# Row tile 2 of a transformer block: x loaded earlier and transposed by DMA, row tile 3 through ScalarE's queue, first Q weights behind two transposes, two transpose banks as accumulators

## The chip, the cores and the metric

The kernel runs on one core of a Trainium2 chip. The time is the device time of one execution in microseconds (us); executions of one kernel in one batch can differ by up to 2 us (the kernel before, batch 2: 690.77 to 692.77), and the 95% intervals below reach about 0.8 us to either side, so with five rounds a difference of about 1 us in 691 can just be told from none. For every run I also look at the mean clock that was granted to TensorE (1.0 is full speed).

## The reference, cut to what matters

```python
def _layernorm(x, axis=-1, eps=1e-5): ...
x = A_x                                              # 2048 x 1024, bf16
h = x + attention(_layernorm(x) @ wqkv) @ wo         # 32 heads, causal, window of 256
h2 = h + silu(_layernorm(h) @ w1) @ w2               # hidden size 3584
```

The change touches only the beginning: the normalization of the first 512 rows ("block 0", four row tiles of 128) and their projection to V, before their projection to Q and K.

## The kernel before: the parts that matter

The matmuls of this kernel read the normalized rows in transposed form (`lhsT=lnT_b[0]...`), so the rows have to be transposed first. A V group is eight matmuls of 512 columns, one for each K tile (128 of the 1024 columns of x), that add up in one accumulator bank; the root of a tile is the square root in its normalization, on ScalarE. For block 0 the kernel transposes row tiles 0, 1 and 2 on TensorE (`turn_first`) so as to start early, and tile 3 by a DMA transpose (`ln_transpose`). Tiles 0 and 1 are multiplied before they are normalized in full and scaled afterwards; their normalized form, which Q and K need, is transposed a second time, by DMA.

```python
def ln_transpose(xt, dst, j):                       # DMA transpose, issued by SyncE
    nc.sync.dma_start_transpose(out=dst[:, :, j * P:(j + 1) * P], in_=xt)

# loads, in the order in which they are issued
load_x(0, 0)
load_x(0, 1, nc.scalar)
load_wqkv(2 * D, 4, (nc.sync, nc.scalar))            # first V weights, four quarters
load_x(0, 2)
load_wqkv(2 * D + 512, 2)                            # second V weights, two halves
load_x(0, 3)
load_wqkv(0)                                         # first Q weights, 1 MB
...
v_group(0, 0, 0, hold, place({...}))                 # V, tile 0, transposes of 0 and 1 in between
turn_first(1, 3, x_mid[1], dve)
...
v_group(0, 1, 0, hold)                               # V, tile 1
pair = [next_acc() for _ in range(2)]                # V, second half of tiles 0 and 1
for k in range(0, KT, 4):
    for j in range(2):
        for kt in range(k, k + 4):
            if k and j:
                turn_first(2, kt - k, x_ring[2], act)    # tile 2 transposed on TensorE
                ...
            nc.tensor.matmul(pair[j], ...)
...
for j in (3, 0, 1):
    ln_transpose(x_ring[j], lnT_b[0], j)
for c0 in (D, 512, D + 512):
    load_wqkv(c0)                                    # the other Q and K weights
v_group(0, 2, 0, act); v_group(0, 2, 1, act)         # V, tile 2
v_group(0, 3, 0, act); v_group(0, 3, 1, act)         # V, tile 3
# then qk_group(0, ...): Q and K of block 0, which read all four tiles
```

Two terms recur below. An issue is the time in which an engine's sequencer hands a transfer to a queue; a landing is the time at which the transfer's semaphore is complete. SyncE's queue takes both the loads and the DMA transposes, in the order of the code.

The softmax here doesn't subtract the row's maximum and nothing guards it: scores larger than these inputs give would overflow.

## Time and profile before

| what | value |
|---|---|
| time, median of 3 runs | 691.15 us (691.08 to 691.35) |
| span of the profiled execution | 688.9 us, granted clock 1.000 (device time 690.64, a fast one) |
| Q/K projections of block 0 start | 21.09 us |
| first Q weights: issued, landed | 6.95, 13.80 us |
| DMA transpose of tile 3: issued, landed | 14.65, 17.50 us |
| of tile 0 | 16.11, 18.83 us |
| of tile 1 | 17.43, 20.20 us |
| next 1 MB of weights: issued, landed | 18.75, 24.21 us |

How to read it: TensorE is busy from one end to the other, so the question for any change here is when the Q/K projections can start; from there on nothing is different. The last thing that they need is the transpose of tile 1, and it lands 0.9 us before they begin. The lines themselves stand in the prediction. One line that I looked up there but did not use as I should have is shown here; it is the view of transfers in a short stretch, with the operation, KB and the median time from issue to landing:

```profile
r_w<-in_A_wqkv_dram SPq DMA_DIRECT2D x1, 1024.0 KB, 5.5
```

A megabyte of weights with no other load in front of it, issued at 18.75 behind tile 1's transpose (landed at 20.20), took 5.5 us to land.

### The profile page before, as it was taken

To read this page: it belongs to the slowest core of one execution; us is meant where nothing else is said; L and a number is where in the kernel's file an instruction comes from. 1 tells how busy PE (TensorE), PEld (TensorE's weight loads), DVE (VectorE), ACT (ScalarE), POOL (GpSimd) and SP (SyncE) were. 2 spreads that over 40 slices of the span, in tenths; PEclk is the share of its full clock that TensorE was granted. 3 is DMA by queue.
4 is the path that set the end of the run, shared out by engine and by line. 5 is a ranking of instruction groups with operands and counts; after the bars stand their busy time and mean duration, and the time that the engine had idled before them with its cause. 6 is when DMAs were issued, how large, how long until landed. Compare 5 with 4: busy or idle time off the path is not lost.

```text
span 688.9 us, 14243 instructions
## 1 busy us (share of the span) xinstructions
PE 685.2 (99%) x6011; PEld 342.3 (50%) x6011; DVE 291.2 (42%) x613; ACT 244.2 (35%) x464; POOL 160.8 (23%) x295
## 2 busy tenths in 40 slices
PE   9999999999999999999999999999999999999998
PEld 4445555555555555544444444444444444444445
DVE  5267647744444449444316133342233251333111
ACT  7326666666667666421300033300133100233000
POOL 1006666566666656400000000000000000000000
PEclk9999999999999999999999999999999999999999
DMA  7832231126241889871023310022300123100110
GB/s 259 275 64 69 40 85 57 25 63 186 71 131 21 257 252 272 199 267 40 23 88 112 84 39 0 1 91 70 85 0 1 21 96 90 39 1 1 30 39 24
DMA packets 78641, 61.48 MB, mean 89 GB/s; under 512 B 52465, under 2 KB 62705, under 8 KB 78577
## 3 DMA queue, kind: packets, MB, share of 16 engines
q1 hardware_dynamic: 77888, 59.78, 30.2%
q8 instruction: 47, 0.77, 0.4%
q10 hardware_dynamic: 688, 0.79, 0.3%
q14 instruction: 18, 0.14, 0.1%
HBM read 39.85 MB, written 8.39 MB: 70 GB/s over the span
## 4 chain that ended last, share of the span: by engine, by line
PE 99%; DVE 0%; issue 0%
PE hacc L669 19%; PE hacc L706 18%; PE acc L250 17%; PE acc L706 11%; PE acc L669 9%; PE acc L240 7%; PE acc L271 7%; PE o_ps L383 5%; PE sc L303 3%; PE hacc L271 2%; PE sc L355 1%; PE o_ps L240 1%; PE o_ps L167 1%; PE sc L329 1%; PE acc L525 0%; PE o_ps L525 0%
## 5 line engine op out<-in xcount | busy, mean ns | idle before, releaser
L373 POOL TENSOR_SCALAR_AFFINE_SELECT r_e<-r_e 128x512 bf16<-128x512 bf16 (+1 forms) x288 | 157.8, 563 | 123.9 <-ACT r_e L363 60.8
L706 PEld LDWEIGHTS <-r_a 128*128 128x128 bf16 x952 | 90.9, 98 | 103.0
L669 PEld LDWEIGHTS <-r_w 128*128 128x128 bf16 x896 | 87.3, 98 | 104.8
L706 PE MATMUL hacc<-r_a 128*128 128x512 bf16 (+2 forms) x616 | 122.5, 360 | 0.0
L669 PE MATMUL hacc<-r_e,r_w 128*128 128x512 bf16 x456 | 100.9, 379 | 0.0
L315 ACT ACTIVATE r_e<-sc 128x768 bf16<-128x768 f32 x96 | 78.2, 814 | 47.9 <-PE sc L303 47.9
L678 ACT ACTIVATE r_n<-hacc 128x512 f32<-128x512 f32 x30 | 17.9, 597 | 178.9 <-PE hacc L669 178.9
L250 PEld LDWEIGHTS <-r_w 128*128 128x128 bf16 x512 | 47.1, 98 | 55.0 <-issue 1.0
L706 PE MATMUL acc<-r_a 128*128 128x512 bf16 x336 | 74.0, 379 | 0.0
L252 DVE CAST r_a<-acc 128x512 bf16<-128x512 f32 x56 | 38.7, 692 | 57.7 <-PE acc L250 57.4
L250 PE MATMUL acc<-r_t,r_w 128*128 128x512 bf16 x256 | 59.6, 380 | 0.0
L250 PE MATMUL acc<-r_w 128*128 128x512 bf16 x256 | 57.8, 380 | 0.0
L383 PEld LDWEIGHTS <-r_e 128*128 128x128 bf16 x1440 | 47.4, 96 | 17.9
L669 PE MATMUL acc<-r_e,r_w 128*128 128x512 bf16 x216 | 49.1, 379 | 0.0
L271 PE MATMUL acc<-r_o,r_a 128*128 128x512 bf16 x208 | 48.7, 380 | 0.0
L383 PE MATMUL o_ps<-r_a,r_e 128*128 128x33 bf16 x1440 | 48.1, 178 | 0.0
L721 DVE SCALAR_TENSOR_TENSOR r_t<-hacc,r_t 128x512 bf16<-128x512 f32 (+2 forms) x22 | 14.0, 635 | 56.7 <-PE hacc L706 56.7
L316 ACT ACTIVATE r_e<-sc 128x256 bf16<-128x256 f32 x96 | 37.6, 392 | 0.0
L271 PEld LDWEIGHTS <-r_a 128*128 128x128 bf16 x256 | 23.4, 98 | 26.9
L721 DVE SCALAR_TENSOR_TENSOR r_t<-acc,r_t 128x512 bf16<-128x512 f32 x12 | 8.3, 692 | 64.2 <-PE acc L706 64.2
L679 DVE SCALAR_TENSOR_TENSOR r_a<-r_n,hacc 128x512 bf16<-128x512 f32 x30 | 20.6, 687 | 33.0 <-ACT r_n L678 33.0
L669 PE MATMUL hacc<-r_a,r_w 128*128 128x512 bf16 x144 | 33.0, 379 | 0.0
(100 smaller groups left out, 539.6 us busy)
## 6 DMA issues: line engine op xcount, KB each, us to landing
r_w<-in_B_w_dram SPq DMA_DIRECT2D x8, 896.0 KB, 5.2
r_a<-in_B_w_dram SPq DMA_DIRECT2D x7, 1024.0 KB, 7.5
r_w<-in_A_wqkv_dram SPq DMA_DIRECT2D x4, 1024.0 KB, 7.8
h_dram<-r_t SPq DMA_DIRECT2D x16, 256.0 KB, 3.1
r_t<-h_dram SPq DMA_DIRECT2D x16, 256.0 KB, 2.8
out_dram<-r_t SPq DMA_DIRECT2D x31, 128.0 KB, 1.7
r_o<-in_A_x_dram SPq DMA_DIRECT2D x15, 256.0 KB, 4.6
r_e<-h_dram SPq DMA_DIRECT2D x3, 1024.0 KB, 5.7
```

The lines of the kernel that those rows point to most:

```text
L240: nc.tensor.matmul(acc, lhsT=lnT_b[b % 2][:, kt, j * P:(j + 1) * P], rhs=wv[:, kt, c * 512:(c + 1) * 512], start=(kt == 0), stop=(kt == KT ...
L250: nc.tensor.matmul(acc, lhsT=wqk[:, kt, col0:col0 + P], rhs=lnT_b[b % 2][:, kt, :], start=(kt == 0), stop=(kt == KT - 1))
L252: copy(out=(qT, kT)[which][b][:, g, :], in_=acc)
L271: nc.tensor.matmul(acc, lhsT=qT[b][:, g, j * P:(j + 1) * P], rhs=wo[:, g, c * 512:(c + 1) * 512], start=(g == 0), stop=(g == G - 1))
L303: nc.tensor.matmul(sc[hh // 2][half * 64:half * 64 + 64, hh % 2, col:col + qb - qa], lhsT=kT[t // 4][r0:r0 + DH, g, k0:k0 + 64], rhs=qT[b] ...
L315: nc.scalar.activation(out=tri[:, :, :, 64:256], in_=both, func=ACT.Exp, scale=scale)
L316: nc.scalar.activation(out=e[:, 1024:1280].rearrange("p (h q) -> p h q", q=P), in_=bank[:, :, 192:320], func=ACT.Exp, scale=scale)
L373: nc.gpsimd.affine_select(out=dst, in_=src, pattern=[[0, n] for n in dst.shape[1:-1]] + [[sgn, P]], compare_op=ALU.is_ge if upper else ALU ...
L383: nc.tensor.matmul(o_ps[pair][:, qt * 2 + hh, 0:VW], lhsT=chunk_of(i, bank, piece, pair, hh), rhs=v[:, b * 4 + kt, g * 4 + pair * 2 + hh, ...
L669: nc.tensor.matmul(acc, lhsT=w1[:, kt, ft * P:(ft + 1) * P], rhs=ln2T[b][:, kt, :], start=(kt == 0), stop=(kt == KT - 1))
L706: nc.tensor.matmul(acc[:, 0:c1 - c0], lhsT=gT[:, ft, j * P:(j + 1) * P], rhs=w2[ft // 4][:, ft % 4, c0:c1], start=(ft == 0), stop=(ft == F ...
L721: nc.vector.scalar_tensor_tensor(out=t_out[j % 2][:, c0:c1], in0=acc[:, 0:c1 - c0], scalar=0.5, in1=t_in[j % 2][:, c0:c1], op0=ALU.mult, o ...
```

## The change

The intent is to take the eight transposes of tile 2 off TensorE, to have tile 2 and tile 3 ready sooner, and to spread the accumulators of the V groups over more banks. For this, x of tile 2 goes ahead of the third quarter of the first V weights on SyncE's queue (the second and fourth go through ScalarE's); tile 3's x is loaded through ScalarE's queue, after tile 2's root; the first Q weights move behind the transposes of tiles 2 and 3 on SyncE's queue. The copies of tile 1's transposes go from VectorE to ScalarE.

```diff
-    load_wqkv(2 * D, 4, (nc.sync, nc.scalar))
-    load_x(0, 2)
+    load_wqkv(2 * D, 4, (nc.sync, nc.scalar), load_x)    # x of tile 2 after the second quarter
     load_wqkv(2 * D + 512, 2)
-    load_x(0, 3)
-    load_wqkv(0)
 ...                                                      (helper changes cut)
+    def turn_root():
+        turn(1, 1)
+        ln_root(st, rs, 2)
+        load_x(0, 3, nc.scalar)
 ...
-    turn_first(1, 3, x_mid[1], dve)
+    turn(1, 3)
+    ln_recip(rs, 2)
+    ln_norm(x_ring[2], st, rs, 2)
+    ln_transpose(x_ring[2], lnT_b[0], 2)
 ...                                                      (statistics of tile 3 moved up, cut)
+    ln_norm(x_ring[3], st, rs, 3)
+    ln_transpose(x_ring[3], lnT_b[0], 3)
+    load_wqkv(0)
     v_group(0, 1, 0, hold)
     scaled(0)
     scaled(1)
+    acc_banks += [t[:].bitcast(F32) for t in tp_ps[2:]]
+    acc_n[0] = 2
     pair = [next_acc() for _ in range(2)]
 ...
-                if k and j:
-                    turn_first(2, kt - k, x_ring[2], act)
 ...
-    for j in (3, 0, 1):
         ln_transpose(x_ring[j], lnT_b[0], j)              # now in the loop over tiles 0 and 1
```

More of the change, by code (lines that the diff above doesn't have):

```diff
@@ L135, in load_x, with load_wqkv @@
         queue.dma_start(out=x_ring[(b % 2) * 4 + j], in_=x2d[(b * 4 + j) * P:(b * 4 + j + 1) * P, :])
-    def load_wqkv(c0, parts=1, queues=(nc.sync,)):
+    def load_wqkv(c0, parts=1, queues=(nc.sync,), second=None):
         dst = wqk[:, :, c0:c0 + 512] if c0 < 2 * D else wv[:, :, c0 - 2 * D:c0 - 2 * D + 512]
@@ L141, in load_wqkv @@
             queues[k // n % len(queues)].dma_start(out=dst[:, k:k + n, :], in_=wqkv_v[:, k:k + n, c0:c0 + 512])
+            if second and k == n:
+                second(0, 2)
     warm = view(r_e, 0, P)
@@ L479, in place @@
     def place(at):
-        return lambda kt: turn_first(*at[kt], x_mid[at[kt][0]], (act, dve)[at[kt][0]]) if kt in at else None
+        return lambda kt: at[kt]() if kt in at else None
     acc_banks += [o[:].rearrange("p a b -> p (a b)") for o in o_ps]
@@ L496 @@
     nc.vector.tensor_tensor(out=mean[:, 2:3], in0=mean[:, 0:1], in1=mean[:, 1:2], op=ALU.add)
-    turn_first(0, 0, x_mid[0], act)
-    turn_first(0, 1, x_mid[0], act)
+    ln_stats(x_ring[2], st, 2)
+    turn = lambda j, h: turn_first(j, h, x_mid[j], act)
+    turn(0, 0)
+    turn(0, 1)
     for i in range(2):
         busy(2)
-    v_group(0, 0, 0, hold, place({1: (0, 2), 3: (0, 3), 5: (1, 0), 6: (1, 1), 7: (1, 2)}))
-    turn_first(1, 3, x_mid[1], dve)
+    def turn_root():
+        turn(1, 1)
+        ln_root(st, rs, 2)
+        load_x(0, 3, nc.scalar)
+    v_group(0, 0, 0, hold, place({1: lambda: turn(0, 2), 3: lambda: turn(0, 3), 5: lambda: turn(1, 0), 6: turn_root, 7: lambda: turn(1, 2)}))
+    turn(1, 3)
+    ln_recip(rs, 2)
+    ln_norm(x_ring[2], st, rs, 2)
+    ln_transpose(x_ring[2], lnT_b[0], 2)
     for j in range(2):
@@ L506 @@
         root_first(j)
-    ln_stats(x_ring[2], st, 2)
-    ln_root(st, rs, 2)
+    ln_stats(x_ring[3], st, 3)
+    ln_root(st, rs, 3)
     ln_recip(rs, 0)
     ln_recip(rs, 1)
-    ln_recip(rs, 2)
-    ln_norm(x_ring[2], st, rs, 2)
+    ln_recip(rs, 3)
+    ln_norm(x_ring[3], st, rs, 3)
+    ln_transpose(x_ring[3], lnT_b[0], 3)
+    load_wqkv(0)
     v_group(0, 1, 0, hold)
@@ L519 @@
             for kt in range(k, k + 4):
-                if k and j:
-                    turn_first(2, kt - k, x_ring[2], act)
-                    if kt == k:
-                        ln_stats(x_ring[3], st, 3)
-                        ln_root(st, rs, 3)
                 nc.tensor.matmul(pair[j], lhsT=lnT_b[0][:, kt, j * P:(j + 1) * P], rhs=wv[:, kt, 512:1024], start=(kt == 0), stop=(kt == KT - 1))
-    norm_first(0)
-    norm_first(1)
-    ln_recip(rs, 3)
-    ln_norm(x_ring[3], st, rs, 3)
     for j in range(2):
+        norm_first(j)
         nc.scalar.activation(out=v[:, j, 16:32, 0:DH], in_=pair[j].rearrange("p (h d) -> p h d", d=DH), func=ACT.Identity, scale=rs[:, j:j + 1])
-    for j in (3, 0, 1):
         ln_transpose(x_ring[j], lnT_b[0], j)
```

## The prediction

> **What bounds the kernel now.** I read the page first: busy time by engine and the chain that ended last.
>
> ```profile
> PE 685.2 (99%) x6011; PEld 342.3 (50%) x6011; DVE 291.2 (42%) x613; ACT 244.2 (35%) x464; POOL 160.8 (23%) x295
> ...
> PE 99%; DVE 0%; issue 0%
> ```
>
> TensorE is busy in 685.2 of 688.9 us and the chain is TensorE from end to end, at a granted clock of 1.000. So any time that the change saves or adds on TensorE's stream passes to the end one for one, and nothing on another engine counts unless TensorE waits for it. The diff only touches the first 21 us (row block 0: V projection and its transposes), about 3% of the time. I therefore went on to TensorE's timeline there (start, duration, both in us; matmuls overlap, so I use starts and not durations).
>
> ```profile
> 6.92 0.59 PE L240 MATMUL acc<-r_w 128*128 128x512 bf16 x2
> 7.35 0.28 PE L218 MATMUL tp<-ident,r_e 128*128 128x128 bf16 x2
> 7.46 0.38 PE L240 MATMUL acc<-r_w 128*128 128x512 bf16 x1
> 7.68 0.28 PE L218 MATMUL tp<-ident,r_e 128*128 128x128 bf16 x2
> 7.91 0.38 PE L240 MATMUL acc<-r_w 128*128 128x512 bf16 x1
> ...
> 8.56 1.89 PE L240 MATMUL o_ps<-r_w 128*128 128x512 bf16 x8
> 10.29 1.03 PE L525 MATMUL o_ps<-r_w 128*128 128x512 bf16 x4
> ...
> 12.88 0.28 PE L218 MATMUL tp<-ident,r_o 128*128 128x128 bf16 x2
> 12.99 0.38 PE L525 MATMUL acc<-r_w 128*128 128x512 bf16 x1
> ...
> 14.19 1.89 PE L240 MATMUL acc<-r_w 128*128 128x512 bf16 x8
> ...
> 21.09 27.79 PE L250 MATMUL acc<-r_w 128*128 128x512 bf16 x128
> ```
>
> What to see: eight 512-wide matmuls take 10.29 - 8.56 = 1.73 us, 0.216 each. The eight transposes of row tile 2 (the r_o ones) lie between the last four matmuls before 14.19. The Q/K projections begin at 21.09, and they need all four row tiles transposed.
>
> Then SyncE's queue, because it orders the loads and the DMA transposes.
>
> ```profile
> 1.26 0.93 SPq L141 DMA_DIRECT2D r_w<-in_A_wqkv_dram  x2
> 2.23 0.47 SPq L135 DMA_DIRECT2D r_o<-in_A_x_dram  x1
> 2.74 1.37 SPq L141 DMA_DIRECT2D r_w<-in_A_wqkv_dram  x2
> 4.97 0.34 SPq L135 DMA_DIRECT2D r_o<-in_A_x_dram  x1
> 6.95 0.37 SPq L141 DMA_DIRECT2D r_w<-in_A_wqkv_dram  x1
> 14.65 4.04 SPq L206 DMA_TRANSPOSE r_w<-r_o  x3
> 18.75 1.87 SPq L141 DMA_DIRECT2D r_w<-in_A_wqkv_dram  x3
> ```
>
> The three transposes cost the queue 1.35 us each; the view of landings gives 2.9, 2.8 and 2.7 us from issue to landing, so the last lands at about 17.4 + 2.7 = 20.1, before 21.09. In between, the DMA engines' share in 40 slices of 14.5 to 21.0 us shows the data of each as a burst of six slices of 0.16 us, about 0.95 us, starting 1.3 us after its issue:
>
> ```profile
> DMA  0000000008999990049999940299999600962935
> ```
>
> **What the Trainium skill says.** "DMA: Bandwidth & Descriptors", section "Queues, rings and completion order": on one DMA engine the descriptors of one queue are taken in ring order. The trace agrees as far as landings go: pieces of SyncE's queue issued at 1.75, 2.23 and 2.74 land at 7.0, 7.8 and 9.15. The same page, "Issuing engines are not separate DMA queues": issuing from ScalarE saves only the sequencer's time, the data share the same 16 engines; here the engines move some 385 GB/s without a gap from 2.5 to 13.3 us whichever queue issues, so a load only comes earlier by pushing another later. "VectorE: DVE Perf Modes", "The three transpose paths", gives 390 ns for a 128x128 transpose on TensorE and 1309 ns by DMA. This trace has a far smaller TensorE figure in the stream (below), and that one decides. "TensorE: Matmul & The Clock Gate", "Wait — 56ns, not 53.3ns?", gives 55.6 and 215.7 ns from start to start for 128 and 512 columns on a warm array; the trace agrees (12.88 to 12.99 for two transposes, 0.216 for a matmul).
>
> **The change part by part.**
>
> 1. Transposes of tile 2 leave TensorE. From 12.88 to 14.19 are 1.31 us; four matmuls alone are 4 x 0.216 = 0.86. Saved: 0.45 us, on the path. This is all that can be gained in steady flow.
>
> 2. x tile 2 goes ahead of the third quarter of the first V weights (K tiles 4 and 5) in SyncE's queue. Both are 256 KB. Before, that quarter is issued at about 1.75 and lands 5.2 later, at 7.0; x tile 2 at 2.23 and 5.6 later, 7.8. Swapped, the quarter lands at 7.8. TensorE reaches K tile 4 at 7.13 (the second of the pair at 6.92), so it now waits until about 7.83: +0.70. Before, it lost 0.12 later, at 7.91, waiting for the last quarter (the two transposes from 7.68 are over at 7.79; that quarter lands at 1.99 + 5.9 = 7.9), and this wait is swallowed. Net +0.58: the second V group starts at 9.14 instead of 8.56.
>
> 3. The eight copies of transposed tiles 0 and 1 are all on ScalarE (0.37 us each, 0.30 to 0.33 back to back). The last four, with the root of tile 2 (0.29), run from about 8.37 to 10.0. The second V group reads the third copy at its K tile 4 (9.14 + 0.86 = 10.0; copy done 9.67) and the fourth at 10.44 (done 10.0). No wait, margin about 0.3.
>
> 4. Row tile 2: x lands at 7.0, statistics 1.5 us on VectorE, root, reciprocal, normalization (0.55) until about 10.0; the DMA transpose then lands at about 12.9. Its group starts at 9.14 + 8 x 0.216 + 16 x 0.216 = 14.33 (before 14.19). No wait. The extra accumulators keep that group from waiting for an eviction, which before was no wait either.
>
> 5. Row tile 3: the new order on ScalarE puts its root after the two squares (1.28 each) and roots, at about 13.0; normalized by 13.9, so its transpose is issued at 13.95 rather than 14.65 and lands at 16.85. Needed at 14.33 + 3.46 = 17.79. No wait.
>
> 6. The first Q weights, 1 MB, are issued at 6.95 before, and now only after tile 3's transpose, at 13.95 + 1.26 = 15.2, ahead of the transposes of tiles 0 and 1. At 385 GB/s they occupy the engines for 2.7 us, from about 16.55 (1.35 after issue, as the load at 18.75 had it) to 19.3. The two transposes behind them in ring order take 0.95 each: 21.15, and landing another 0.4: about 21.55. TensorE, without a wait, would want the Q/K projections at 14.33 + 32 x 0.216 = 21.24. So it waits some 0.3, and with a little for the semaphore starts at about 21.65 to 21.7.
>
> Sum: 21.7 - 21.09 = +0.6 us; put by parts, -0.45 + 0.58 + 0.45. After that TensorE runs as before: the next weights (issued around 18.4) are wanted 6.9 us later and land by 25, and x of block 1 comes near 32 us, where VectorE has over 2 us of slack. 691.15 + 0.6 = 691.75.
>
> **Rivals.** (a) Only the quarter's wait exists: the transposes mix with the Q weights or the transfer is quicker than I think, and tile 1 lands in time: -0.45 + 0.58, 691.3. For it: the margin in step 6 is 0.3 us, less than the error of my start times. Against it: the total data ahead of the last transpose is fixed by ring order. (b) Only the late Q weights matter: if TensorE didn't wait at K tile 4, everything up to the transposes moves 0.58 forward and about 0.4 of wait remains at the Q/K start: 691.1. Against it: the first V group was already following the landings to within 0.2 us. (c) Neither wait: 690.7, the intent of the change. (d) Transposes and copies disturb one another more than by bytes, or tile 3 comes late for its group: another 0.5 to 1 us, 692.3 to 692.8.
>
> **Range and chances.** Most weight lies on my sum and (a); the range 690.7 to 692.6 covers (a) to the mild form of (d). 2% would be 13.8 us. All that the change can move is the first 21 us, and the waits named are below 1 us each, so within 2% has 0.98.
>
> **What would show it.** In the changed profile: no transposes of r_o on TensorE; a gap of 0.6 to 0.7 us before the fifth matmul of the first V group, released by the weights' DMA; second V group at 9.1; tile 2's group at 14.3 with no DMA wait; the Q/K start at 21.6 to 21.7 with a wait released by a DMA transpose; from there the same distance to the end. It is wrong if the quarter lands before 7.2, if the Q/K start is at 21.0 or sooner, or if the time between Q/K start and the end changes by more than 0.3 us.

## The result, and the profile after

| | before | after |
|---|---|---|
| time, median, same rounds | 691.19 us (690.87 to 691.47, 6 runs) | 693.49 us (692.91 to 695.53, 6 runs) |
| ratio | | 1.0037, 95% interval 1.0024 to 1.005 |

A ratio is the mean time of one kernel's fast runs over that of the other's in the same rounds, so it is not quite the ratio of the medians quoted. The interval lies clear of 1: the change costs 2.3 us, and 693.49 lies outside the predicted range of 690.7 to 692.6. So the size was wrong: 0.6 us expected, 2.3 measured.

The page of the changed kernel, busy time and chain:

```profile
PE 686.1 (99%) x6003; PEld 342.0 (49%) x6003; DVE 290.0 (42%) x609; ACT 244.1 (35%) x464; POOL 160.8 (23%) x295
...
PE 98%; DMA 2%; SPq 0%; ACT 0%; issue 0%; DVE 0%
```

TensorE runs eight instructions fewer (the transposes are gone), and yet DMA now stands in the chain with 2%. That is where to look. TensorE's timeline in the first part (start, duration in us, what it is, and in brackets the idle time before it with what ended it):

```profile
7.17 0.38 PE L239 MATMUL acc<-r_w 128*128 128x512 bf16 x1
8.55 0.38 PE L239 MATMUL acc<-r_w 128*128 128x512 bf16 x1 [1.00 <-DMA r_w<-in_A_wqkv_dram]
...
9.86 1.89 PE L239 MATMUL o_ps<-r_w 128*128 128x512 bf16 x8
...
15.04 1.89 PE L239 MATMUL tp<-r_w 128*128 128x512 bf16 x8
...
20.22 1.89 PE L239 MATMUL o_ps<-r_w 128*128 128x512 bf16 x8
24.10 29.47 PE L249 MATMUL acc<-r_w 128*128 128x512 bf16 x128 [1.99 <-DMA r_w<-r_o]
```

There are two waits. The first (1.00) is for the quarter of V weights that x of tile 2 overtook. The second (1.99) stands in front of the Q/K projections and is released by a DMA transpose. And there is a third thing that the prediction had not thought of: the 128 matmuls of that first Q/K stretch last 29.47 us, against 27.79 before. The view of windows says why (columns: stretch, its length, busy time of the five engines with their instructions, granted TensorE clock, DMA share, GB/s):

```profile
24.10:26.00 1.90, 1.90 (x6) 0.76 (x7) 0.00 (x0) 0.00 (x0) 0.00 (x0) 0.62 1.05 369
26.00:28.00 2.00, 2.00 (x6) 0.70 (x5) 0.00 (x0) 0.58 (x1) 0.00 (x0) 0.51 1.09 385
28.00:30.00 2.00, 2.00 (x11) 0.93 (x10) 0.49 (x1) 0.00 (x0) 0.00 (x0) 1.00 1.09 377
```

After the wait the granted clock falls to one half for about 3.4 us and then returns. That costs 29.47 - 27.79 = 1.7 us in this execution, which was the slowest of the six (695.53); the other five show a clock of 1.0 and lie between 692.91 and 693.61. So the drop does not make the median. The transfers do. SyncE's queue (start and duration of the issues):

```profile
10.78 5.20 SPq L205 DMA_TRANSPOSE r_w<-r_o  x2
16.03 0.57 SPq L141 DMA_DIRECT2D r_w<-in_A_wqkv_dram  x1
16.79 5.09 SPq L205 DMA_TRANSPOSE r_w<-r_o  x2
21.93 2.85 SPq L141 DMA_DIRECT2D r_w<-in_A_wqkv_dram  x3
```

The order is that of the code: tiles 2 and 3, Q weights, tiles 0 and 1. The transfers that begin between 16.0 and 16.9 take, from issue to landing (last number of each line):

```profile
r_w<-in_A_wqkv_dram SPq DMA_DIRECT2D x1, 1024.0 KB, 6.0
r_w<-r_o SPq DMA_TRANSPOSE x1, 6.3
```

The Q weights take 6.0 us where I had put 4.5, and the transpose of tile 0 behind them 6.3 where a free one takes 2.7 to 2.9. The profiled execution had a late start besides (its first x tile landed at 4.06, not 3.52). I therefore ran the changed kernel again.

### The profile page after: what moved, and what is told of

It is laid out like the page before. It is cut to its first block, busy times and chain, and to the rows that moved or that the text cites.

```text
span 693.8 us, 14223 instructions
## 1 busy us (share of the span) xinstructions
PE 686.1 (99%) x6003; PEld 342.0 (49%) x6003; DVE 290.0 (42%) x609; ACT 244.1 (35%) x464; POOL 160.8 (23%) x295
## 3 DMA queue, kind: packets, MB, share of 16 engines
q10 hardware_dynamic: 832, 1.05, 0.4%
## 4 chain that ended last, share of the span: by engine, by line
PE 98%; DMA 2%; SPq 0%; ACT 0%; issue 0%; DVE 0%
PE hacc L674 19%; PE hacc L711 17%; PE acc L249 17%; PE acc L711 10%; PE acc L674 9%; PE acc L270 7%; PE acc L239 7%; PE o_ps L382 5%; PE sc L302 3%; PE hacc L270 1%; DMA r_w<-in_A_wqkv_dram 1%; PE sc L354 1%; DMA r_w<-r_o 1%; PE sc L328 1%; PE tp L534 0%; PE tp L239 0%
## 5 line engine op out<-in xcount | busy, mean ns | idle before, releaser
L249 PE MATMUL acc<-r_w 128*128 128x512 bf16 x256 | 59.5, 388 | 2.0 <-DMA r_w<-r_o 2.0
```

What stands on the lines that cost most here:

```text
L249: nc.tensor.matmul(acc, lhsT=wqk[:, kt, col0:col0 + P], rhs=lnT_b[b % 2][:, kt, :], start=(kt == 0), stop=(kt == KT - 1))
```

## The experiments

All outputs are right. Four batches ran; the kernel before had medians of 691.01, 691.25, 690.97 and 691.48 us in them, and every ratio is to the runs of before of the same batch.

### e0: the changed kernel again (batch 2)

No edit.

> The changed kernel once more, on the same chip as the three below: about 693.4 at a clock of 1.000. If the wait of 2 us at the Q/K start makes the clock drop in a share of the executions, some show 0.997 and 695 to 695.5; if the drop of the first profile was chance, none do.

Measured: 693.83 us (693.46 to 694.24, 5 runs), ratio 1.0033 (1.002 to 1.0046), clock 1.0 in every run. The Q/K line of its timeline:

```profile
23.91 27.79 PE L249 MATMUL acc<-r_w 128*128 128x512 bf16 x125 [2.11 <-DMA r_w<-r_o]
```

At full clock (27.79, as before) the wait is still there: the loss of 2.3 to 2.6 us comes without any drop of the clock. This clean execution gives the balance. The second V group starts at 9.55 (before 8.56): +0.99, of which 0.23 is there before the overtaken quarter plays a part (the first V matmul at 6.11, before 5.88). From there to tile 2's group at 14.73 are 5.18 us, before 5.63: -0.45. From there to the Q/K start are 9.18 us; the four groups need 6.91 of them (8 x 4 x 0.216), which was all they took before: +2.27. Together +2.81, and the Q/K start moved by 23.91 - 21.09 = 2.82.

### e7: only the place of the Q weights (batch 2)

```diff
     ln_transpose(x_ring[2], lnT_b[0], 2)
+    load_wqkv(0)
 ...
     ln_transpose(x_ring[3], lnT_b[0], 3)
-    load_wqkv(0)
```

> The changed kernel with only the first Q weights moved, to between the transposes of tiles 2 and 3; x tile 2 stays ahead of the weights' quarter. Theory L: the wait at the Q/K start (2.0 us in the profile) goes; a wait of some 0.5 us for tile 3's transpose, which now stands behind the 1 MB, comes; the quarter's wait of 1.0 stays: 691.9 to 692.4. Were the Q weights harmless there, 693.4 would stay.

Measured: 691.84 us (691.34 to 692.45, 5 runs), ratio 1.0006 (0.9994 to 1.0017). Its timeline around the Q/K start:

```profile
18.65 1.90 PE L239 MATMUL acc<-r_w 128*128 128x512 bf16 x8 [0.41 <-DMA r_w<-r_o]
20.39 1.89 PE L239 MATMUL o_ps<-r_w 128*128 128x512 bf16 x8
22.12 8.15 PE L249 MATMUL acc<-r_w 128*128 128x512 bf16 x36
```

No wait is left in front of the Q/K projections; a smaller one, 0.41 us, appears before tile 3's group, whose transpose now goes behind the load. One line moved, and 693.83 - 691.84 = 2.0 us of the loss are gone. All other parts of the change, gains and losses together, come to the 0.6 us that are left (691.84 - 691.25; the interval includes none), about what I had predicted for the whole.

### e2: the kernel before, with only the Q weights late (batch 1)

```diff
     load_x(0, 3)
-    load_wqkv(0)
 ...
     for j in (3, 0, 1):
         ln_transpose(x_ring[j], lnT_b[0], j)
+        if j == 3:
+            load_wqkv(0)
```

> The kernel before with only the first Q weights moved to between tile 3's transpose and those of tiles 0 and 1. Theory L: the whole loss and more appears, since tile 3's transpose is issued at 14.65 as in the changed kernel's profile (14.75): last transpose lands near 24, the Q/K start moves from 21.1 to about 23.5 to 24, 693.6 to 694.1 us. Rival S: 691.2 to 691.8, no more than my predicted byte count (2.7 us on the wire plus two transposes) gives.

Measured: 695.94 us (694.73 to 697.83, 6 runs), ratio 1.0069 (1.0056 to 1.0083); five of the six runs show a clock of 0.995 to 0.998, and the one at 1.0 is the fastest, 694.73.

```profile
24.83 5.40 PE L249 MATMUL acc<-r_w 128*128 128x512 bf16 x17 [3.21 <-DMA r_w<-r_o]
```

The late load alone makes the kernel before slower by 3.7 us at full clock (694.73 - 691.01, a single execution against a median), more than I had expected. The wait was 3.21 us; the load took 6.43 us and the transpose of tile 1 landed at 24.70. So the move makes a loss without the rest of the change, as e7 shows that the rest makes hardly any without the move.

### e10: the kernel before, with only x of tile 2 ahead (batch 2)

```diff
-    load_wqkv(2 * D, 4, (nc.sync, nc.scalar))
-    load_x(0, 2)
+    load_wqkv(2 * D, 4, (nc.sync, nc.scalar), load_x)
```

> The kernel before with only x tile 2 moved ahead of the third quarter of the first V weights. My step 2 (the two pieces of 256 KB swap places, +0.58 us): 691.6 to 691.8. If the quarter is delayed by more than its bytes, as the gap of 1.0 to 1.5 us in the changed kernel's and the first run's profile suggests: 692.0 to 692.4. If the swap costs nothing: 691.1.

Measured: 691.79 us (691.36 to 692.22, 5 runs), ratio 1.0005 (0.9993 to 1.0017). The difference of medians is 0.54, the predicted one was 0.58. The interval includes zero, so the size is consistent with step 2 rather than proved by the times. In the trace, the wait for the overtaken quarter is 0.64 us, but another of 0.48 us, for the quarter before it, comes first, and the second V group starts at 9.61, 1.05 us later than in the profile of before. That is more than the medians show: single executions differ here by as much as the effect.

### e5: the Q weights behind all four transposes (batch 2)

```diff
     ln_transpose(x_ring[3], lnT_b[0], 3)
-    load_wqkv(0)
 ...
-    for c0 in (D, 512, D + 512):
+    for c0 in (0, D, 512, D + 512):
```

> The changed kernel with the first Q weights issued after all four transposes. The transposes then land by about 20 us and the Q/K start waits for the weights alone. Theory ramp (loads from HBM run slowly for their first 1.5 us or so when none ran before, whatever stands behind them): 1 MB issued near 18.6 lands near 24.3, as late as now, 693.2 to 693.8. Theory mix (the load was slow because transposes were being issued and queued behind it): 2.7 us on the wire, lands near 23.1, 692.2 to 692.6.

Measured: 695.25 us (693.78 to 696.22, 6 runs), ratio 1.005 (1.0037 to 1.0064). Two runs have a clock of 1.0 (693.78 and 693.86), four 0.997 or 0.998.

```profile
24.29 3.47 PE L249 MATMUL acc<-r_w 128*128 128x512 bf16 x8 [2.39 <-DMA r_w<-in_A_wqkv_dram]
```

The executions at full clock and the landing fit the theory of the ramp. Now the releaser is the load itself: issued at 18.74, landed at 24.24, 5.50 us, as the load of 18.75 in the kernel before. All four transposes have landed long before (tile 1's at 20.18, 1.4 us after the load's issue). So the load is slow even with no transpose behind it, and with transposes behind it 0.6 us slower still (6.14 in e0).

### e13: no pause in the loads before it (batch 3)

A theory for the slow load: no load had been running for a while, so it starts cold. Here two x tiles of block 1 are loaded just ahead of it, through ScalarE's queue.

```diff
     ln_root(st, rs, 3)
+    load_x(1, 0, nc.scalar)
+    load_x(1, 1, nc.scalar)
 ...
-    for j in range(4):
+    for j in range(2, 4):
         load_x(1, j)
```

> The changed kernel with two of the four x loads of block 1 (512 KB) moved from after the weights to ScalarE's queue right after the root of tile 3, so that loads from HBM are flowing when the first Q weights start. If the slow start is due to the pause in loads before it, those weights land in about 4.5 us from issue instead of 6.1, and the Q/K start moves about 1.3 us forward: 692.2 to 692.7. If it is due to something else (the weights' own addresses, the transposes before), landing stays near 6 us and the time at 693.5 or above.

Measured: 694.32 us (692.99 to 696.17, 4 runs, two of them at a clock of 0.998 or less), ratio 1.0046 (1.0027 to 1.0065). The Q weights took 6.10 us, and the Q/K start is where it was:

```profile
23.87 6.42 PE L249 MATMUL acc<-r_w 128*128 128x512 bf16 x29 [1.93 <-DMA r_w<-r_o]
```

Of the four executions the two at full clock took 692.99 and 693.52. The two x loads landed at 16.10 and 16.93, so loads were flowing when the weights were issued at 15.74, and the landing came no sooner for it. The start did change: from 17.5 to 19.0 us the engines moved 210 to 283 GB/s (61 to 231 in e0), and a later dip took the gain away. The pause is not what makes the landing late; whether it has a part in the slow start stays open.

### e15: another megabyte in the same place (batch 4)

As e7, with the four x loads of block 1 (1 MB in all) where the Q weights had been.

```diff
     ln_transpose(x_ring[2], lnT_b[0], 2)
+    load_wqkv(0)
 ...
     ln_transpose(x_ring[3], lnT_b[0], 3)
-    load_wqkv(0)
+    for j in range(4):
+        load_x(1, j)
```

> The changed kernel with the first Q weights between the transposes of tiles 2 and 3 (as in e7, 691.8), and the four x loads of block 1 (also 1 MB, in rows of 2 KB) put where the late Q weights were, ahead of the transposes of tiles 0 and 1. Theory A: any 1 MB load issued there takes 6 us and holds the transposes behind it up: the transpose of tile 1 lands at 23.5 to 24, Q/K projections start at 23.6 to 24 after a wait of 1.5 to 2 us, about 693.6. Rival B: only the 1 KB pieces of the weights, or one large load, start slowly: the loads land about 4.5 us after issue, the transpose of tile 1 by 22, Q/K start at about 22.2, 691.8.

Measured: 693.49 us (693.33 to 694.13, 5 runs), ratio 1.003 (1.0018 to 1.0043), clock 1.0 throughout.

```profile
23.63 27.79 PE L249 MATMUL acc<-r_w 128*128 128x512 bf16 x125 [1.49 <-DMA r_w<-r_o]
```

The time and the wait are those of theory A. The x loads, issued from 15.52 to 17.09, land at 19.08, 19.96, 20.56 and 21.50, and the transpose of tile 1 at 23.49. What costs is a megabyte in that place, not these weights. But the x loads are late for another reason than the Q weights were. They stood behind the Q weights (landed at 17.45) and tile 3's transpose (18.46), and once these were through they moved at full rate within about a microsecond (last column GB/s):

```profile
18.00:18.50 0.50, 0.15 (x1) 0.00 (x0) 0.00 (x0) 0.31 (x1) 0.00 (x0) 1.00 0.98 279
18.50:19.00 0.50, 0.49 (x3) 0.26 (x4) 0.00 (x0) 0.48 (x2) 0.00 (x0) 1.00 1.03 393
```

So this run does not show that any load there starts slowly, and rival B is not excluded as a cause of the slow start.

### e16: the Q weights in four loads (batch 4)

```diff
-    load_wqkv(0)
+    load_wqkv(0, 4)
```

> The changed kernel with the late Q weights as four loads of 256 KB in place of one of 1 MB, same place and order. If the slow start comes with the size of one load, the last quarter lands by about 20 and the transpose of tile 1 by 22: a Q/K wait of 0.3 us, about 692.0. If it is the place that counts (an idle queue in front, transposes behind), nothing changes: landing at 21.9 to 22.5, tile 1 at 23.8, Q/K wait of 2 us, 693.5 to 694; the three more issues may add some 0.3.

Measured: 693.95 us (693.02 to 695.03, 5 runs), ratio 1.0036 (1.0024 to 1.0049). The quarters, issued from 15.47, land at 18.40, 19.08, 21.23 and 21.91; the transpose of tile 1 at 23.91.

```profile
24.05 27.79 PE L249 MATMUL acc<-r_w 128*128 128x512 bf16 x125 [2.55 <-DMA r_w<-r_o]
```

Four loads of 256 KB are no sooner done than one of 1 MB: the size of a single load is not the reason.

### e9: the Q weights on ScalarE's queue (batch 3)

```diff
         load_x(0, 3, nc.scalar)
+        load_wqkv(0, 1, (nc.scalar,))
 ...
     ln_transpose(x_ring[3], lnT_b[0], 3)
-    load_wqkv(0)
```

> The changed kernel with the first Q weights issued on ScalarE's queue right behind x tile 3, near 9.5 us, so they stand in front of no transpose in ring order and follow loads without a pause. Theory ring order and ramp: they land near 14.5, the wait at the Q/K start goes; tile 2's transpose shares the engines with them and lands about a microsecond later (near 14.3, wanted at 14.7), so mostly the quarter's wait is left: 691.2 to 691.8. If sharing the engines hurts transposes as much as standing behind in the ring, tile 2's group waits 1 us or more: 692.2 and up.

Measured: 692.96 us (692.83 to 693.66, 5 runs), ratio 1.0026 (1.0012 to 1.004).

```profile
16.44 1.90 PE L239 MATMUL tp<-r_w 128*128 128x512 bf16 x8 [1.70 <-DMA r_w<-r_o]
```

There is no wait before Q/K, but tile 2's group now waits 1.70 us. The load was issued at 9.32 on ScalarE's queue and landed at 15.36; the transpose of tile 2, issued at 10.30 on SyncE's queue, landed at 16.39, after 6.09 us instead of 2.86. Here the other queue did not let the transpose past the load.

### e1: the Q weights early, as before (batch 1)

```diff
     load_wqkv(2 * D + 512, 2)
+    load_wqkv(0)
 ...
     ln_transpose(x_ring[3], lnT_b[0], 3)
-    load_wqkv(0)
```

> The changed kernel with one thing undone: the first Q weights (1 MB) are issued early again, right behind the V weights. Theory L (the late Q weights in front of the last two transposes make the loss): the wait at the Q/K start goes, but tile 2's transpose now stands behind 1 MB in SyncE's queue; the quarter's wait stays. About 691.3 to 692.0, that is at least 1.4 us faster than the changed kernel's 693.5. Rival S (the swap of x tile 2 and the weights' quarter, and the later chain of tile 3 behind it, make the loss): still over 692.8. Rival T (the clock drop of the profiled run makes it): follows whether a clock under 1.000 is granted.

Measured: 692.70 us (692.56 to 693.59, 5 runs), ratio 1.0025 (1.0013 to 1.0037).

```profile
8.80 0.38 PE L240 MATMUL acc<-r_w 128*128 128x512 bf16 x1 [1.51 <-DMA r_w<-in_A_wqkv_dram]
...
15.85 1.90 PE L240 MATMUL tp<-r_w 128*128 128x512 bf16 x8 [0.40 <-DMA r_w<-r_o]
...
20.31 1.90 PE L240 MATMUL acc<-r_w 128*128 128x512 bf16 x8 [0.84 <-DMA r_w<-r_o]
```

A miss. Early in the queue the megabyte is no longer in front of tiles 0 and 1, but it is in front of tile 2 (its transpose: issued 11.02, landed 15.80) and beside tile 3's x (issued 9.66, landed 14.85, against 11.74 in e0). The wait for the quarter (1.51 us) is longer here than in any other run. The wait for transposes moves; it does not vanish. This also says why the change moves the load at all.

### e3: x of tile 2 in its old place (batch 1)

```diff
-    load_wqkv(2 * D, 4, (nc.sync, nc.scalar), load_x)
+    load_wqkv(2 * D, 4, (nc.sync, nc.scalar))
+    load_x(0, 2)
```

> The changed kernel with x tile 2 loaded after the four quarters of the first V weights, as before. Theory L: the quarter's wait (0.6 to 1.0 us in the first V group) goes, but the Q/K start still waits for the last transpose; it comes sooner only as far as tile 3's transpose is issued sooner (at most 0.6): 692.8 to 693.5. Rival S: 690.7 to 691.3.

Measured: 693.93 us (693.61 to 697.27, 6 runs, two at a clock of 0.997), ratio 1.005 (1.0034 to 1.0066).

```profile
10.99 1.04 PE L240 MATMUL o_ps<-r_w 128*128 128x512 bf16 x4 [0.78 <-ACT r_w L219]
```

A miss: no gain. The root of tile 2 stands in ScalarE's order ahead of the last two copies of tile 1's transposes. When x of tile 2 comes later, the root waits for its statistics, the copies wait behind the root, and TensorE waits 0.78 us for a copy. The early x and the place of the root belong together. Nor did the wait for the quarter go in this execution: 0.59 us are left, since the quarter landed at 7.84 in its old place too (6.93 in the profile of before). Before Q/K it waits 2.56 us.

### e6: both, Q weights between and x of tile 2 in its old place (batch 1)

The edits of e7 and e3 together.

> x tile 2 in its old place and the first Q weights issued between the transposes of tiles 2 and 3, so they stand in front of neither tile 2 nor tiles 0 and 1. Theory L: both waits go and the saving of eight transposes is left: 690.6 to 690.9, faster than the kernel before by 0.3 to 0.5 us. If tile 3's transpose comes late behind the 1 MB (wanted at about 17.2 us), up to 691.5. Rival S: also about 690.7, so this run tells the theories apart only together with the third.

Measured: 691.81 us (691.58 to 692.95, 5 runs), ratio 1.0012 (1.0 to 1.0024). Its waits are again 0.6 us for a copy on ScalarE and 0.55 for the transpose of tile 3; before Q/K there is none, and they start at 22.49. Above the expected 690.6 to 690.9, for the reason found in e3 and for the wait for tile 3, which the expectation had allowed for.

### e12 and e11: the Q weights in two halves (batch 3)

```diff
+    def half_q(k):
+        nc.sync.dma_start(out=wqk[:, k:k + 4, 0:512], in_=wqkv_v[:, k:k + 4, 0:512])
 ...
     load_wqkv(2 * D + 512, 2)
+    half_q(0)
 ...
     ln_transpose(x_ring[2], lnT_b[0], 2)
+    half_q(4)
 ...
-    load_wqkv(0)
```

> The changed kernel with only the first Q weights split as in the run before (x tile 2 ahead of the weights' quarter as in the change): the swap's 0.5 less the transposes' 0.45, so about the time of the kernel before, 691.1 to 691.6. Still at 691.8 or more if tile 3's transpose waits behind the second half.

Measured for e12: 692.33 us (691.29 to 692.65, 5 runs), ratio 1.0012 (0.9999 to 1.0024). The waits up to Q/K shrink to 0.64 and 0.16 us, and Q/K start at 21.46. But the profiled execution has another wait of 1.3 us much later, in the first part of the MLP (for an accumulator that VectorE has to free), that I can't connect with the edit; e3 has a smaller one of the kind (0.7), e6 and e5 have 0.6 and 0.4 on the same line without a releaser, and before, after, e0 and e7 have none.

e11 adds the edit of e3 and moves the root of tile 2 behind the last copy.

```diff
-        ln_root(st, rs, 2)                # in turn_root
 ...
     turn(1, 3)
+    ln_root(st, rs, 2)
```

> An attempt to beat both kernels: x tile 2 in its old place; on ScalarE all four copies of tile 1 before the root of tile 2; the first Q weights in two halves of 512 KB, one behind the V weights, one between the transposes of tiles 2 and 3. If no wait is left, the kernel before less the eight transposes: 690.6 to 690.9. If tile 2's or tile 3's transpose comes late behind the halves: up to 691.6.

Measured for e11: 691.88 us (691.49 to 692.97, 5 runs), ratio 1.0011 (0.9998 to 1.0023). The wait for the copy is gone. The one that remains is 0.57 us for tile 3: its x, issued at 8.27, shared the engines with the first half and landed at 12.84.

### e14: as e11, with x of tile 3 ahead of the first half (batch 4)

```diff
     load_wqkv(2 * D + 512, 2)
+    load_x(0, 3)
     half_q(0)
 ...
-        load_x(0, 3, nc.scalar)           # in turn_root
```

> A last attempt at a faster kernel: as e11 (x tile 2 in its old place, the first Q weights in two halves), with x tile 3 issued on SyncE's queue ahead of the first half, so that it doesn't share the engines with it. Expected: x tile 3 lands at about 11, no wait for the transpose of tile 3 (0.57 in e11), Q/K start at 20.9 to 21.2, 690.6 to 691.2. Rival: the first half then lands later and delays the transpose of tile 2, whose group waits 0.3 to 0.6 us instead: 691.5 to 692.

Measured: 690.96 us (690.6 to 691.43, 5 runs), ratio 0.9992 (0.9978 to 1.0006).

```profile
17.82 1.90 PE L245 MATMUL acc<-r_w 128*128 128x512 bf16 x8 [0.22 <-DMA r_w<-r_o]
...
21.29 27.79 PE L255 MATMUL acc<-r_w 128*128 128x512 bf16 x125
```

x of tile 3 lands at 11.25, the wait for tile 3 is down to 0.22 us, and there is none before Q/K. This version is as fast as the kernel before. Its median is lower by 0.5 us, but the interval includes 1, and in the profiles its Q/K start (21.29) is no earlier than that of before (21.09), so no gain is shown.

## Why the prediction was wrong

**The frame held.** TensorE's stream sets the end, only the beginning moves, and what delays the Q/K start delays the end: the start moved by 2.82 us in e0 and the median by 2.6.

**Step 1 (-0.45) held.** In the trace of e0 the stretch that lost its transposes is shorter by 5.63 - 5.18 = 0.45 us. I had no run that makes this part alone.

**Step 2 (+0.58) was right in kind; its size is not settled.** e10 has +0.54 in the medians, with an interval that includes zero. In e0 the second V group starts 0.99 us later, and the overtaken quarter lands at 8.20, not 7.8. In the profiles with the early x the wait for the quarter goes from none (e15) to 1.51 us (e1), and e3 has 0.59 without the early x. The landings that the step read were also rounded: 6.93 and 7.88 in the trace, 7.0 and 7.8 in the text.

**Step 3 held** for the kernel as changed: no wait for a copy. e3 shows how thin it is: with x of tile 2 later the same order costs 0.78 us.

**Steps 4 and 5 held in their verdicts,** no wait for tiles 2 and 3. Their times were early by 0.4 to 0.5: the transpose of tile 2 landed at 13.32 in e0 (12.9 predicted), that of tile 3 was issued at 14.43 (13.95).

**Step 6 failed, and this is the error.** It says of the first Q weights "At 385 GB/s they occupy the engines for 2.7 us, from about 16.55 (1.35 after issue, as the load at 18.75 had it) to 19.3". The load was issued at 15.71 in e0, half a microsecond late because of step 5; that much is a small shift. Then it took 6.14 us to land, where the step's figures give 1.35 + 2.7 + 0.4 = 4.5. The part behind it was right: from its landing to that of tile 1's transpose are 23.77 - 21.85 = 1.9 us, as predicted (two transposes of 0.95). So of the 2.2 us between the predicted landing of tile 1 (21.55) and the measured one, 0.5 came with the issue and 1.6 with the load. The step failed in the cost of that load: I had put a steady rate on a transfer that does not begin at that rate. The view of windows shows it, for the changed kernel (last column GB/s, the one before it the DMA share):

```profile
17.50:18.00 0.50, 0.50 (x4) 0.21 (x3) 0.00 (x0) 0.06 (x1) 0.00 (x0) 1.00 0.90 82
...
18.50:19.00 0.50, 0.50 (x4) 0.26 (x3) 0.00 (x0) 0.30 (x1) 0.00 (x0) 1.00 0.60 174
19.00:19.50 0.50, 0.50 (x4) 0.22 (x3) 0.00 (x0) 0.48 (x2) 0.00 (x0) 1.00 0.98 340
```

The engines count as busy, 0.60 and 0.90 of the time in the two lines, but move 82 and 174 GB/s before they reach 340. (The packets of the load in e0's trace say how both can be: some of the first 1 KB packets take up to 1.4 us each, where one of the steady part takes 46 ns.) And the kernel before had the same in its own load at 18.75:

```profile
20.00:20.50 0.50, 0.50 (x4) 0.25 (x3) 0.00 (x0) 0.40 (x1) 0.00 (x0) 1.00 0.74 119
20.50:21.00 0.50, 0.50 (x4) 0.24 (x3) 0.00 (x0) 0.00 (x0) 0.00 (x0) 1.00 0.71 137
21.00:21.50 0.50, 0.50 (x4) 0.19 (x2) 0.00 (x0) 0.21 (x1) 0.00 (x0) 1.00 0.98 344
```

The profile that I predicted from held the figure: 5.5 us from issue to landing. With it, step 6 would have put tile 1 at 22.55 and the time at about 692.7, and more than half of the miss would have gone. I read that load's start and not its landing.

**Of the rivals,** (d), "Transposes and copies disturb one another more than by bytes", comes nearest and ends at 692.8; it, too, is too small, and e5, with 5.5 us and no transpose behind the load, leaves about 0.6 us to it. (a), (b) and (c) fall with the wait of 2.11 us before Q/K.

**The test of the last sentence.** "from there the same distance to the end" is off by 0.4 us in e0 (692.1 - 23.91 against 688.9 - 21.09), a little over the 0.3 that the prediction allowed, and fails by 1.9 in the first profile of the changed kernel, nearly all of it the clock's drop. I had not foreseen this. It appeared in some executions of the kernels with a profiled wait of 1.9 us or more before Q/K: one of six after the change, none of five in e0, five of six in e2 (3.21 us), four of six in e5 (2.39), two of six in e3, two of four in e13, one of five in e16; and in none of the kernels with shorter waits. (A clock of 0.999, in e14 and e16, is no such drop where it was profiled: there the clock fell in the last microsecond of the program.) It widens the spread, and raises the medians of e2, e5 and e13.

**What is shown and what is open.** Shown: the late load is what costs (e7 takes 2.0 us away, e2 alone adds 3.7), through the transposes behind it. Another megabyte in the same place costs it too (e15). That the load takes 6 us and not 4.5 is not the size of a single load (e16), and not only the transposes behind it (e5: still 5.5 us); ending the pause before it did not help (e13). Open: why the load runs slowly for its first microsecond or two. Transposes just in front of it are not enough: the x loads of e15 follow one too. Two explanations fit the traces and no run separates them. The slow loads (e0, e5, e7, e16 and the one at 18.75 before) had little or nothing left in the queue when they could begin, whereas the x loads of e15, and the Q weights in their early place in the kernel before, had been queued behind unfinished work. Or it is the 1 KB pieces of the weights, where x has 2 KB rows: the first x loads of the kernel before, which also find an idle queue, go from 41 to 369 GB/s within a microsecond and a half. I found no edit that starts this load at full rate except keeping it among other loads, as the kernel before does. Open too: the late wait in e12 and e3.

## What to carry to other kernels

Take a transfer's duration from a landing of the same kind in the trace, with the same things in front of it and behind it, not from bytes over the steady rate. When a load is moved in a queue, ask for everything behind it by when it must land: here the load itself was just in time (it landed at 21.85 in e0, where TensorE had been free from 21.80), and the transposes behind it were not. And a wait of a couple of microseconds on TensorE may cost nearly as much again in the clock that follows (1.7 us after a wait of 1.99 here).

## What the Trainium skill lacked or had wrong

- "DMA: Bandwidth & Descriptors", section "Latency and other measured facts", speaks of a fixed cost of about 2 us for a DMA. With 1 MB at the 385 GB/s of this trace (2.7 us) that would be 4.7 us, as an estimate; single 1 MB loads that began after or among transposes took 5.2 to 6.4 us here (5.47 before, 5.50 in e5, 6.14 in e0, 6.43 in e2). The page has no figure for the slow start.
- The same page, section "Queues, rings and completion order", says that an engine takes turns between queues packet by packet. In e9 the transpose on SyncE's queue, issued 0.98 us after the load on ScalarE's, landed 1.03 us after that load, in 6.09 us and not 2.86. Turns between the two were not to be seen: from 11.6 to 14.0 us only packets of ScalarE's queue ran. Whether the engines took no turns or had no work from the other queue yet, the trace does not tell.
- No page says how long a DMA transpose takes behind a load: 6.43 us in e0, where the free one took 2.72 to 2.86. The issue itself lengthens: 2.4 to 2.7 us on SyncE against 1.23 to 1.34.
- "TensorE: Matmul & The Clock Gate", section "What's actually happening", gives half clock after an idle window of about 3.4 us. Here less sufficed. In the four profiles with a drop (after, e2, e3, e5) the clock records show the half clock for 3.41 us, from 20.48 us (six times 3.41) after the clock had first risen to full. Cut into stretches of 3.41 us from that rise, the waits with a drop have 1.99, 3.01, 2.40 and 2.39 us inside one stretch, and the long waits without one have at most 1.93 (e13), 1.80 (e16) and 1.38 (e0), the last two because they lie across the edge of two stretches. So about 2 idle us in a stretch of 3.4 separate the seven profiles; this fits them and was not tested further. The drop lasted 3.4 us and cost 1.7.
